# Two feed-forward layers behind agent attention, float32: the first block's second-layer products in full fp32, the block of 448 tokens second, and part of the late weights' decoding on GpSimd

## The chip, the cores and the metric

One NeuronCore of a Trainium2 chip runs the whole kernel. The metric is the device time of one execution in microseconds. Names: TensorE (PE in the profile; PEld is its weight load), VectorE (DVE), ScalarE (ACT), GpSimd (POOL), SyncE (SP, which issues all DMAs of this kernel).

## What is computed

12480 tokens of 128 channels, 49 agents, two feed-forward layers with 2048 hidden units. In short:

```python
agent_v = sm(agents, k) @ v                       # softmax over the 12480 keys
x = sm(q, agents) @ agent_v                       # softmax over the 49 agents
h = x @ w_in1;  g = where(h >= 1, h, where(h <= -1, 0, (h + 1)**2 / 4));  y = g @ w_out1
h = y @ w_in2;  g = s * relu(h)**2 + b;           out = g @ w_out2
```

Inputs and outputs are float32; the four weight matrices arrive as 64-bit floats, seen as pairs of 32-bit words.

## The kernel before

**Blocks and steps.** Tokens go through in 25 blocks whose widths stand in `widths`: 256, then 23 of 512, then 448. Tokens are the columns. A layer's block is worked in 8 steps (`JP`) of two chunks of 128 hidden units, so a step's tile is 128 x 2w. Layer-1 step n is block n // 8; layer 2 runs `D` = 11 steps behind layer 1.

**One step.** `H` makes the hidden values in PSUM. `relu`, `square` (ScalarE) and, in layer 1, `cap` (VectorE, L745) make g. Products run in fp32r, so g is split: `hi` rounds it to fp32r (`gh`, on ScalarE L754 or VectorE L756, chosen by `PAT1`, `PAT2`) and `lo` subtracts (`gl`, VectorE, L761). `O` sums three products per chunk, `wh*gh + wl*gh + wh*gl`, in one PSUM bank (`y` for layer 1, `o` for layer 2). A step for which `short` is true skips `hi` and `lo`, and `O` takes one product in full fp32 with the unsplit weights (`w32`) per chunk; before, these are the layer-1 steps below `FP` = 12. In the records a full fp32 product stands as two matmuls.

**First-layer scores.** The first layer's input weights and the attention's values are fused ahead (`weights`, `awh`, `awl`, L599 to L606), so that `H` of layer 1 takes the softmax over the agents directly. Blocks 0 and 1 (`t < QB`) take two products per chunk with `awh` and `awl`; later blocks take one (L707) and four small tiles side by side (L715), for which `px` is filled by DMA. From block 3 on, softmaxes are made for two blocks at a time: `pair_scores`, a transpose on VectorE (`pair_turn`, L266), the `pair_steps`, and at their end `spread`, which issues 32 DMAs on SyncE out of `turned` (L293). The next pair's transpose writes `turned` again and so waits for them.

**Weights.** `decode` turns eight pieces of 1024 columns (A: second output weights, B: first input, C: first output, D: second input) into float32 in six steps, numbered 0 to 5: `scale_down` (L364 or L368), `tail` (L373), `join` (L378), `sign` (L383), `high` (L389), `low` (L392). All eight are scaled on ScalarE (`MACT`); all `low` run on VectorE.

**Order.** Each engine takes its instructions in the order in which the program issues them. Up to the fused weights that order is written out in `SEQ`, from there to layer-1 step 13 in `RAMP` (tokens: `H0` is layer 1's H, `h0` layer 2's, `R S M O` relu, square, cap and output product of layer 1, `r s G l o` those of layer 2, `A0.5` step 5 of piece A0, `z` a step of an early block's softmax, `=F1`, `=G1` high and low part of a quarter of the fused weights, `x` a column sum of the second output weights). Behind that `steady` weaves the lists in `PAIR`, one for each engine, under the dependencies given to `add`. `LOADS` is the order of the loads; the loads of keys and values share seven buffers, those of weight pieces three.

Of the kernel before, what the change touches and what calls it, by code (L numbers as in the profile page):

```python
# [18 lines left out]
def kernel(  # L19
# [55 lines left out]
        "B0 k0 k1 k2 k3 k4 k5 k12 k6 k7 k8 k9 k10 k11 v0 q0 v1 v2 v3 C1 v4 C0 B1 v5 v6 v7 q1 v8 v11 v9 v10 D0 "  # L75
        "v12 A0 q2 A1 D1"
    )
    RAMP = (
# [5 lines left out]
    )  # L84
    MACT = "B0 C1 C0 B1 D0 A0 A1 D1".split()
    WORD = "B0 C1 C0 B1 D0 A0 A1 D1".split()
    NR, FP = 14, 12
# [14 lines left out]
    widths = [256] + [512] * 23 + [448]  # L102
# [44 lines left out]
    w32, turned = shared[:, :DFF], shared[:, 2 * TB:]  # L147
    ptok = [packed[:, i * TB:(i + 1) * TB].rearrange("p (c n) -> p c n", n=P) for i in range(NPT)]
# [119 lines left out]
    def pair_steps(v):  # L268
# [10 lines left out]
        def spread():  # L279
# [4 lines left out]
            for j, t in enumerate(x for x in pair_blocks(v) for _ in range(2)):  # L284
# [6 lines left out]
                for dst, main in ((pt_t[t], True), (px_t[t], False)):  # L291
                    for c in range(4):
                        nc.sync.dma_start(  # L293
                            out=dst.bitcast(F32)[c * RG:(c + 1) * RG, x0:x0 + n], in_=src[:, c if main else 4]
                        )
# [51 lines left out]
    def decode(dec, src, dst, dst_h, dst_l, name):  # L347
# [12 lines left out]
        def scale_down():  # L360
            if not t:
                begin()
            if name in MACT:
# [3 lines left out]
            else:  # L367
                nc.vector.tensor_scalar_mul(t["y"].bitcast(F32), t["hi"].bitcast(F32), 2.0 ** -112)  # L368
# [22 lines left out]
        def low():  # L391
            nc.vector.tensor_tensor(  # L392
# [46 lines left out]
    def agents_values(pro, dec, wi1):  # L439
        pieces.update({  # L440
            "A": (w_out2, None, flat(wo2h), flat(wo2l)), "B": (w_in1, wi1, None, None),
# [11 lines left out]
        avt = pro.tile([P, P], F32, name="avt")  # L453
# [266 lines left out]
    def short(layer, n):  # L720
        return layer == 1 and n < FP
# [5 lines left out]

    def gv(d, layer, n):
        return d[layer, n][:, :, :blocks[n // JP][1]]

    def relu(layer, n):
        gx[layer, n] = ring("gl", layer, n, F32, GR) if short(layer, n) else ring("x", layer, n, F32, XB)
# [40 lines left out]
    def last_step(first):  # L773

        n = NS - 1
        if first:
            gx[2, n] = ring("x", 2, n, F32, XB)
# [11 lines left out]
    def O(layer, n):  # L789
# [6 lines left out]
        if short(layer, n):  # L796
            x = gx.pop((layer, n))
            ops = [(w32.rearrange("p (k d) -> p k d", d=P), x)]
# [65 lines left out]
    def steady():  # L864
# [19 lines left out]
        for n0 in range(NR, NS + D + D2 + 2, 2):  # L884
            for e, tokens in (PAIR if n0 < NS else TAIL).items():
                for token in tokens:
# [20 lines left out]
                    elif c == "o" and 0 <= m - 2 < NS:  # L907
                        k = m - 2
                        add(("o", k), [("l", k), ("Z", k // JP - 1)], O, 2, k)
# [14 lines left out]
                    elif c == "r" and 0 <= m < NS - 1:  # L924
                        add(("r", m), [("h", m), ("l", m - XB)], relu, 2, m)
# [4 lines left out]
                    elif c in "GC" and 0 <= m - 1 < NS - 1 and (c == "G") == (GH(2, m - 1) == "1"):  # L930
# [66 lines left out]
```

## Time and profile before

| | |
|---|---|
| median of 3 runs | 1059.88 us (1059.49 to 1060.31) |
| the profiled execution | 1058.94 us, of it the span of its instructions 1057.2 us |
| PE busy | 1039.0 us (98%) |
| DVE busy | 965.9 us (91%) |
| ACT busy | 980.5 us (93%) |
| POOL busy | 0.9 us, 7 instructions |
| granted TensorE clock, mean | 0.996 |

The span runs from the first to the last instruction. Matmuls are pipelined: one shows a duration longer than the time to the next one's start, and an engine that is busy throughout may still lose time, so starts are compared. "Idle" in brackets is the engine's idle time ahead of an instruction and what ended it.

### The profile page before, as it was taken

What the parts mean: (1) busy time and instruction counts of PE and PEld (TensorE: products, weight loads), DVE (VectorE), ACT (ScalarE), POOL (GpSimd) and SP (SyncE); (2) the same over time, 40 slices, a digit from 0 to 9 for tenths busy, and PEclk for the clock granted to TensorE, in tenths of its full rate; (3) what the DMA queues carried; (4) which work ended last, traced back from release to release, by engine and by line L of the source; (5) the groups of instructions that cost most, each with busy time, mean ns of one, the idle gap of its engine ahead of it and who ended that gap; (6) DMA issues with size and microseconds to landing.
All of it is one profiled execution on the core that took longest, in us unless ns stands there. A gap on an engine that the chain in (4) does not pass through costs nothing.

```text
span 1057.2 us, 13302 instructions
## 1 busy us (share of the span) xinstructions
PE 1039.0 (98%) x4928; PEld 789.9 (75%) x4928; DVE 965.9 (91%) x1102; ACT 980.5 (93%) x1059; POOL 0.9 (0%) x7
## 2 busy tenths in 40 slices
PE   7899999999999999999999999999999999999998
PEld 3767667777777777777777777777777777777787
DVE  5698989999999999999999999999999999999876
ACT  3798989999999999999999999999999999999986
POOL 0000000000000000000000000000000000000000
PEclk9999999999999999999999999999999999999999
DMA  9940020110110110010010010020020010010000
GB/s 362 385 148 27 14 53 11 34 37 11 26 46 11 24 47 11 22 49 11 20 52 11 18 54 11 14 56 11 13 56 10 12 39 11 11 38 11 1 11 20
DMA packets 32114, 47.68 MB, mean 45 GB/s; under 512 B 7285, under 2 KB 23653, under 8 KB 31409
## 3 DMA queue, kind: packets, MB, share of 16 engines
q1 hardware_dynamic: 32049, 46.83, 14.0%
q8 instruction: 39, 0.64, 0.3%
q14 instruction: 26, 0.21, 0.1%
HBM read 27.58 MB, written 6.39 MB: 32 GB/s over the span
## 4 chain that ended last, share of the span: by engine, by line
PE 90%; DMA 3%; DVE 2%; ACT 2%; SPq 2%; issue 1%; DVEq 0%
PE y L805 26%; PE h L675 25%; PE o L805 24%; PE h L707 8%; PE h L715 4%; SPq L293 1%; DMA k<-in_kT 1%; DMA wu<-in_w_out 1%; PE qs L259 1%; DVE gl L761 1%; PE ks L510 1%; DMA px<-pt 1%; PE av L564 1%; DVE x L745 0%; ACT x L741 0%
## 5 line engine op out<-in xcount | busy, mean ns | idle before, releaser
L761 DVE TENSOR_TENSOR gl<-x,gh 128x1024 fp32r<-128x1024 f32 (+2 forms) x387 | 461.5, 1201 | 10.9 <-ACT gh L754 8.0
L741 ACT ACTIVATE x<-x 128x1024 f32<-128x1024 f32 (+2 forms) x387 | 405.6, 1048 | 11.5
L745 DVE SCALAR_TENSOR_TENSOR x<-h,x 128x1024 f32<-128x1024 f32 (+1 forms) x188 | 228.3, 1215 | 32.8 <-ACT x L741 32.5
L735 ACT ACTIVATE x<-h 128x1024 f32<-128x1024 f32 (+1 forms) x188 | 189.2, 1006 | 19.1 <-PE h L707 12.9
L737 ACT ACTIVATE x<-h 128x1024 f32<-128x1024 f32 (+2 forms) x199 | 197.0, 990 | 8.8 <-PE h L675 6.9
L756 DVE CAST gh<-x 128x1024 fp32r<-128x1024 f32 (+1 forms) x245 | 166.7, 681 | 15.5 <-ACT x L741 14.9
L675 PE MATMUL h<-yh,wi2h 128*128 128x512 f32 (+2 forms) x400 | 155.9, 390 | 1.7 <-ACT x L737 0.9
L805 PE MATMUL y<-gh,wo1h 128*128 128x512 f32 (+1 forms) x376 | 156.2, 415 | 0.0
L805 PE MATMUL o<-gh,wo2l 128*128 128x512 f32 (+2 forms) x400 | 155.5, 389 | 0.0
L675 PE MATMUL h<-yl,wi2h 128*128 128x512 f32 (+2 forms) x400 | 155.3, 388 | 0.0
L675 PE MATMUL h<-yh,wi2l 128*128 128x512 f32 (+2 forms) x400 | 155.3, 388 | 0.0
L805 PE MATMUL o<-gh,wo2h 128*128 128x512 f32 (+2 forms) x400 | 154.6, 387 | 0.0
L805 PE MATMUL o<-gl,wo2h 128*128 128x512 f32 (+2 forms) x400 | 154.0, 385 | 0.2 <-DVE gl L761 0.2
L754 ACT ACTIVATE gh<-x 128x1024 fp32r<-128x1024 f32 (+1 forms) x142 | 147.4, 1038 | 3.0
L805 PE MATMUL y<-gl,wo1h 128*128 128x512 f32 (+1 forms) x376 | 148.0, 394 | 0.5 <-DVE gl L761 0.5
L805 PE MATMUL y<-gh,wo1l 128*128 128x512 f32 (+1 forms) x376 | 147.8, 393 | 0.0
L707 PE MATMUL h<-pt,awm 128*128 128x512 f32 (+1 forms) x368 | 100.7, 395 | 0.3 <-ACT x L737 0.3
L805 PEld LDWEIGHTS y<-gh,wo1h 128*128 128x128 f32 x376 | 70.3, 187 | 33.1 <-issue 14.6
L675 PEld LDWEIGHTS h<-yh,wi2h 128*128 128x128 f32 x400 | 74.9, 187 | 20.2 <-ACT x L737 1.7
L805 PEld LDWEIGHTS o<-gh,wo2h 128*128 128x128 f32 x400 | 75.0, 188 | 17.3
L805 PEld LDWEIGHTS o<-gl,wo2h 128*128 128x128 f32 x400 | 75.2, 188 | 16.8 <-DVE gl L761 0.7
L675 PEld LDWEIGHTS h<-yh,wi2l 128*128 128x128 f32 x400 | 74.8, 187 | 17.2
(124 smaller groups left out, 852.2 us busy)
## 6 DMA issues: line engine op xcount, KB each, us to landing
k<-in_kT SPq DMA_DIRECT2D x12, 512.0 KB
v<-in_v_main SPq DMA_DIRECT2D x12, 512.0 KB, 11.5
out_T<-shared SPq DMA_DIRECT2D x23, 256.0 KB, 2.0
pt<-shared SPq DMA_DIRECT2D x172, 32.0 KB, 1.8
px<-shared SPq DMA_DIRECT2D x172, 32.0 KB, 1.8
qbuf<-in_qT SPq DMA_DIRECT2D x10, 512.0 KB, 3.5
wu<-in_w_in SPq DMA_DIRECT2D x4, 1024.0 KB, 11.2
wu<-in_w_out SPq DMA_DIRECT2D x4, 1024.0 KB
```

The lines of the kernel that those rows point to most:

```text
L259: nc.tensor.matmul(out=sc[j * RG:(j + 1) * RG, g], lhsT=a64[:, g * RG:(g + 1) * RG], rhs=qbuf[:, c0:c0 + QW].rearrange("p (b x) -> p b x", ...
L675: nc.tensor.matmul(out=h[:, i, :w], lhsT=a[:, sl], rhs=r, start=(m == 0), stop=(m == len(ops) - 1))
L707: nc.tensor.matmul(out=out[g], lhsT=awm[:, c * P:(c + 1) * P], rhs=pt_t[t][:, :w], start=not last, stop=last)
L715: nc.tensor.matmul(out=out[g], lhsT=awx[r, q], rhs=px_t[t][r, :w], start=not last, stop=last)
L735: nc.scalar.activation(out=x, in_=h, func=ACTF.Relu, scale=0.5, bias=0.5)
L737: nc.scalar.activation(out=x, in_=h, func=ACTF.Relu)
L741: nc.scalar.activation(out=x, in_=x, func=ACTF.Square)
L745: nc.vector.scalar_tensor_tensor(out=x, in0=h, scalar=1.0, in1=x, op0=ALU.max, op1=ALU.min)
L754: nc.scalar.activation(out=a, in_=x, func=ACTF.Copy)
L756: nc.vector.tensor_copy(out=a, in_=x)
L761: nc.vector.tensor_tensor(out=b, in0=x, in1=a.bitcast(F32), op=ALU.subtract)
L805: nc.tensor.matmul(out=o[:, :w], lhsT=l[:, c, :], rhs=r[:, i, :w], start=(c == 0 and m == 0), stop=(c == KF - 1 and m == len(ops) - 1),)
```

## The change

Five things:

- `short` is now also true for the layer-2 steps of block 0 (`FP2` = 8): no `hi` and `lo` there, and 16 products in full fp32 instead of 48 in fp32r. The second output weights are kept in float32 for it (`w32b`, into which A's `sign` writes). Behind these steps two of the three x buffers of layer 2 are the halves of `w32b`.
- The relu of layer 2 waits for an output product where its buffer was one of these (`before`), and `o` for `t` (the square) instead of `l`.
- `widths` starts 256, 448 and ends with 512.
- `SCALES` and `LOWS` give the engine of two decoding steps by piece, in the order of `PIECES`: A0, A1 and C1 are scaled on GpSimd, B0 on VectorE, the rest on ScalarE; A0, A1 and D0 have their low part subtracted on GpSimd, C0, C1 and D1 on VectorE.
- `SEQ`, `LOADS` and `RAMP` are written anew, with other places for most tokens; `avt` takes the memory of `swap`.

```diff
     LOADS = (
-        "B0 k0 k1 k2 k3 k4 k5 k12 k6 k7 k8 k9 k10 k11 v0 q0 v1 v2 v3 C1 v4 C0 B1 v5 v6 v7 q1 v8 v11 v9 v10 D0 "
-        "v12 A0 q2 A1 D1"
+        "k2 k0 B0 k1 k3 k4 k5 k12 k7 k6 k8 k9 k10 k11 v0 q0 v1 v2 v3 C1 C0 v4 B1 v5 v6 v7 q1 v8 v11 v9 v10 D0 "
+        "v12 A0 q2 D1 A1"
     )
     RAMP = (
-        "H0 =F2 =G1 =F3 z1.6 H1 =G2 =G3 K H2 R0 S0 z1.7 R1 S1 M0 H3 z1.8 R2 S2 O0 R3 A0.3 z1.9 M1 M2 H4 A0.4 S3 "
...
-        "M12 g12 R13 z2.9 S13 h0 X r0 s0 G0 M13 L12 h1 r1 g13 s1 O11 B h2 b p2 l0 r2 G1 o0 l1 P2"
+        "H0 =F3 =G1 z1.6 =F2 =G2 =G3 H1 K R0 S0 H2 M0 z1.7 H3 R1 S1 A0.3 R2 O0 M1 O1 R3 S3 S2 z1.8 z1.9 H4 A0.4 "
...
+        "z2.8 z2.9 R13 S13 g12 X h1 r1 r0 s1 L12 s0 M13 g13 O11 B p2 b h2 r2 o0 P2"
     )
-    MACT = "B0 C1 C0 B1 D0 A0 A1 D1".split()
+    SCALES, LOWS = "G G V S S G S S".split(), "G G V V V V G V".split()
+    PIECES = "A0 A1 B0 B1 C0 C1 D0 D1".split()
...
-    NR, FP = 14, 12
+    NR, FP, FP2 = 14, 12, 8
...
-    widths = [256] + [512] * 23 + [448]
+    widths = [256, 448] + [512] * 23
...
+    w32b = const.tile([P, DFF], F32, name="w32b")
...
-            if name in MACT:
+            on = SCALES[PIECES.index(name)]
+            if on == "S":
                 nc.scalar.activation(
                     out=t["y"].bitcast(F32), in_=t["hi"].bitcast(F32), func=ACTF.Copy, scale=2.0 ** -112
                 )
             else:
-                nc.vector.tensor_scalar_mul(t["y"].bitcast(F32), t["hi"].bitcast(F32), 2.0 ** -112)
+                by = nc.gpsimd if on == "G" else nc.vector
+                by.tensor_scalar_mul(t["y"].bitcast(F32), t["hi"].bitcast(F32), 2.0 ** -112)
...
-            nc.vector.tensor_tensor(
+            by = nc.gpsimd if LOWS[PIECES.index(name)] == "G" else nc.vector
+            by.tensor_tensor(
                 out=dst_l[:, sl], in0=t["f"], in1=dst_h[:, sl].bitcast(F32), op=ALU.subtract
             )
...
-            "A": (w_out2, None, flat(wo2h), flat(wo2l)), "B": (w_in1, wi1, None, None),
+            "A": (w_out2, w32b, flat(wo2h), flat(wo2l)), "B": (w_in1, wi1, None, None),
...
-        return layer == 1 and n < FP
+        return n < (FP if layer == 1 else FP2)
...
+    def x_ring(layer, n):
+        if layer == 1 or n % XB == XB - 1:
+            return ring("x", layer, n, F32, XB if layer == 1 else 1)
+        return w32b[:, n % XB * 2 * TB:(n % XB + 1) * 2 * TB].rearrange("p (b n) -> p b n", b=2)
...
-                        add(("o", k), [("l", k), ("Z", k // JP - 1)], O, 2, k)
+                        add(("o", k), [("t", k) if k < FP2 else ("l", k), ("Z", k // JP - 1)], O, 2, k)
...
-                        add(("r", m), [("h", m), ("l", m - XB)], relu, 2, m)
+                        before = [("o", m - GR) if m < FP2 else ("o", m - XB) if m < FP2 + XB else ("l", m - XB)]
+                        add(("r", m), [("h", m)] + before, relu, 2, m)
```

The new `SEQ` puts C1's scaling (`C1.0`, now GpSimd) right ahead of its join, `E12` ahead of `C1.5` and `t10`, and the second block's scores (`q1`) ahead of `a9`; its end is

```python
        "... q1 V12 a9 a10 V11 a11 a12 z1.0 z1.1 D0.1 n D0.0 T z1.2 H W0 z1.3 "
        "D0.2 z1.4 z1.5 W1 W2 F0 A0.0 D0.3 D0.4 A0.1 G0 W3 A0.2 F1"
```

## Rows read from the trace of the kernel before

**Rows 1.** Busy time by stretch of the span; columns by engine, then granted clock, DMA.

```profile
core 0: us, PE busy (x) PEld busy (x) DVE busy (x) ACT busy (x) POOL busy (x), PEclk, DMA share, GB/s
36.00:40.00 4.00, 3.45 (x44) 2.67 (x40) 4.00 (x7) 4.00 (x8) 0.00 (x0) 1.00 1.02 413
53.00:63.00 10.00, 7.44 (x30) 4.30 (x29) 9.97 (x18) 8.99 (x16) 0.00 (x0) 1.00 0.76 248
63.00:98.00 35.00, 34.98 (x179) 27.66 (x180) 32.14 (x45) 33.52 (x47) 0.00 (x0) 1.00 0.14 43
98.00:128.00 30.00, 28.30 (x158) 20.96 (x157) 29.24 (x40) 26.60 (x34) 0.00 (x0) 1.00 0.08 25
165.00:1020.00 855.00, 855.00 (x3909) 654.89 (x3908) 804.82 (x875) 823.90 (x844) 0.00 (x0) 1.00 0.09 25
```

**Rows 2.** Chain that ended last, in order of time: start us, us, what.

```profile
50.68 1.61 PE av L564 x20
53.57 2.00 PE aw L599 x4
83.53 1.72 PE y L805 x4
85.47 1.38 PE h L675 x12
93.79 6.68 DMA px<-pt
108.21 1.74 DVE gl L761 x2
140.89 1.88 DMA pt<-shared
167.22 1.40 PE h L675 x6
1042.37 1.24 PE o L805 x6
```

**Rows 3.** Timeline of PE: start us, us, instruction, idle before and what ended it.

```profile
58.70 0.39 PE L675 MATMUL h<-pt,awh 128*128 128x256 f32 x1 [0.95 <-DVE awl L606]
...
63.02 0.38 PE L675 MATMUL h<-pt,awh 128*128 128x256 f32 x1 [0.57 <-DVE gl L745]
...
99.70 0.50 PE L715 MATMUL h<-px,awx 19*128 19x512 f32 x3
100.51 0.50 PE L715 MATMUL h<-px,awx 19*128 19x512 f32 x1 [0.31 <-DMA px<-pt]
...
106.90 0.39 PE L675 MATMUL h<-yh,wi2h 128*128 128x256 f32 x1 [0.56 <-ACT x L737]
...
143.66 0.50 PE L675 MATMUL h<-yh,wi2h 128*128 128x512 f32 x1 [0.83 <-DVE shared L266]
...
145.99 0.50 PE L805 MATMUL y<-gl,wo1h 128*128 128x512 f32 x1 [0.20 <-DVE gl L761]
```

**Rows 4.** Waits (us in total, times, longest); SyncE's issues into pt, 90 to 146.

```profile
DVE shared L266 <- DMA pt<-shared: 3.9, 1, 3.9
...
L293 SPq DMA_DIRECT2D pt<-shared x16: 577/589/1370, 124.2 to 142.2; - x16
```

**Rows 5.** Groups by line and shape: count, busy us, mean ns, idle before.

```profile
L364 ACT ACTIVATE wt<-wu 128x1024 f32<-128x1024 f32 x8 | 9.3, 1157 | 1.2 <-DMA wu<-in_w_out 1.2
L761 DVE TENSOR_TENSOR gl<-x,gh 128x512 fp32r<-128x512 f32 x8 | 5.5, 683 | 1.1 <-ACT gh L754 1.1
L754 ACT ACTIVATE gh<-x 128x512 fp32r<-128x512 f32 x6 | 3.8, 628 | 0.1
L392 DVE TENSOR_TENSOR wi2l<-wt,wi2h 128x1024 fp32r<-128x1024 f32 x2 | 2.4, 1221 | 0.1
L756 DVE CAST gh<-x 128x512 fp32r<-128x512 f32 x2 | 0.8, 424 | 0.3 <-ACT x L741 0.3
L831 DVE TENSOR_SCALAR shared<-o,s_sb,bcol 128x448 f32<-128x448 f32 x1 | 0.7, 743 | 0.6 <-PE o L805 0.6
```

**Rows 6.** Groups of POOL, by line and shape.

```profile
masks.py:199 POOL TENSOR_SCALAR_AFFINE_SELECT ident<-ident 128x128 f32<-128x128 f32 x1 | 0.3, 292 | 0.1
```

More of the change, by code (lines that the diff above doesn't have):

```diff
@@ L290, in spread @@
                 src = turned[j * RG:(j + 1) * RG].rearrange("r (c x) -> r c x", x=QW)[:, :, QW - n:]
-                for dst, main in ((pt_t[t], True), (px_t[t], False)):
+                for dst, main in ((pt_t[t], True), (px_t[t], False)) if n else ():
                     for c in range(4):
@@ L452, in agents_values @@
         swap = pro.tile([P, P], F32, name="swap")
-        avt = pro.tile([P, P], F32, name="avt")
+        avt = swap
         sc, tp, tok, av, sw = {}, {}, {}, [], []
@@ L731, in relu @@
     def relu(layer, n):
-        gx[layer, n] = ring("gl", layer, n, F32, GR) if short(layer, n) else ring("x", layer, n, F32, XB)
+        gx[layer, n] = ring("gl", layer, n, F32, GR) if short(layer, n) else x_ring(layer, n)
         x, h = gv(gx, layer, n), gv(hp, layer, n)
@@ L776, in last_step @@
         if first:
-            gx[2, n] = ring("x", 2, n, F32, XB)
+            gx[2, n] = x_ring(2, n)
             gh[2, n] = ring("gh", 2, n, F32R, GR)
@@ L797, in O @@
             x = gx.pop((layer, n))
-            ops = [(w32.rearrange("p (k d) -> p k d", d=P), x)]
+            ops = [((w32 if layer == 1 else w32b).rearrange("p (k d) -> p k d", d=P), x)]
         else:
@@ L929, in steady @@
                         add(("t", m - 1), [("r", m - 1)], square, 2, m - 1)
-                    elif c in "GC" and 0 <= m - 1 < NS - 1 and (c == "G") == (GH(2, m - 1) == "1"):
+                    elif c in "GC" and FP2 <= m - 1 < NS - 1 and (c == "G") == (GH(2, m - 1) == "1"):
                         add(("g", m - 1), [("t", m - 1), ("o", m - 1 - GR)], hi, 2, m - 1, c == "G")
-                    elif c == "l" and 0 <= m - 1 < NS - 1:
+                    elif c == "l" and FP2 <= m - 1 < NS - 1:
                         add(("l", m - 1), [("g", m - 1), ("o", m - 1 - GR)], lo, 2, m - 1)
```

17 rows, old and new, of tables (RAMP, SEQ) are left out of this document.

## The prediction

> **What bounds the kernel now.** Start with the busy time by stretch [rows 1]. From 165 to 1020 us TensorE is busy for all of 855 us, VectorE for 804.8 and ScalarE for 823.9: there only TensorE's work counts. The stretch from 63 to 98 is the same (34.98 of 35.00). TensorE is short of full in two places: from 53 to 63 (7.44 of 10.00), and from 98 to 128 (28.30 of 30.00), where VectorE is at 29.24. Ahead of 53 the DMA engines are the limit, with ScalarE full beside them: from 36 to 40 their share is 1.02 and ScalarE has 4.00 of 4.00. Next read the chain that ended last, in order of time [rows 2]: a DMA into px from 93.8 to 100.5, then VectorE's subtractions (L761), then, with SyncE's 32 issues of the first pair's spread (L293) in between, the landing of a DMA of that spread at 142.8, and from there TensorE alone. So up to about 146 us other things than TensorE set the pace; behind that everything is a sum of its products. A microsecond saved ahead of 146 is saved at the end; one saved on VectorE or ScalarE later is worth nothing.
>
> The stops of TensorE [rows 3] say how much there is to win. Between 98 and 147 it stops seven times: once for px, three times for ScalarE's relu (L737), twice for VectorE's subtraction (L761), once for the pair's transpose (L266), which itself waits 3.9 us for the spread's DMAs [rows 4]; the first and the last of these and the pair's stand in the rows. The idle time shown is too small: a 512-column product shows 0.39 but the next one follows after 1.40/6 = 0.233 [rows 2], so each stop loses the idle time shown plus 0.16. At 143.66 that is 0.83 + 0.16, some 0.98. So the six stops other than px lose 0.73, 0.46, 0.39, 0.47, 0.98 and 0.37, together 3.4; the four ahead of 128 are 2.05 of it, the two behind are 1.35. The px stop is 100.51 - 99.70 = 0.8.
>
> **Second-layer products of block 0 in full fp32.** Removed: eight high parts (six on ScalarE at 0.63, two on VectorE at 0.42) and eight low parts on VectorE at 0.68 [rows 5]: ScalarE loses 3.8 us, VectorE 5.4 + 0.8 = 6.3, nearly all of it between 88 and 125, the stretch in which the chain runs through VectorE. Added: 16 products of full fp32 in place of 48. A step's two full products are four records, and at 512 columns these take 1.72 (the first layer's at 83.53 [rows 2]): 0.86 a product, so 0.43 at 256 columns. Three ordinary products of 256 columns take 3 x 1.38/12 = 0.345 [rows 2]. The difference is 0.085 x 16 = **+1.4** us of TensorE, with nothing to hide it.
>
> What the relief gives: the four stops ahead of 128 wait for VectorE or ScalarE, and both lose more work there (6.3 and 3.8) than the stops add up to (2.05). I take nine tenths, **-1.8**. The two stops behind 128 hang on the spread: SyncE needs 0.59 us for each of its 32 DMAs, the 16 for pt among them start from 124.2 to 142.2 [rows 4], and the next pair's transpose waits for the last that reads its place. With less on VectorE the spread comes earlier by up to 3 us while TensorE itself comes about 2 us earlier, so the gap of 1.35 mostly closes: **-1.1**, between 0 and -1.35. The px stop: the copy that feeds its DMAs stood on ScalarE behind two high parts of 0.63, which go; 1.26 earlier against a stop of 0.8, while TensorE also comes to that place a little sooner: **-0.5**, between 0 and -0.8. The new waits of relu for an output product instead of a low part (`("o", m - GR)`, `("o", m - XB)`) I cost at nothing: TensorE's list puts that product ahead of the H whose result the relu needs, so the second wait covers the first. Uncovered, one would cost a step's two products, 0.86.
>
> **Block of 448 second.** Between 512 and 448 columns an ordinary product differs by (1.40 - 1.24)/6 = 0.027 us [rows 2]. The second block has 32 products for its first-layer scores (later blocks 16, and 4 passes of four tiles at once). It saves 32 + 24 ordinary ones at 0.027 and eight full ones at 0.86 x 64/512 = 0.107: 2.37. The last block, now 512, gives back 16 + 4 + 48 at 0.027: 1.84. The second layer's cancels. Net **-0.5**. The drain behind the last product grows by the last evacuation, 0.74 for 448 columns [rows 5], so by 0.74/7: **+0.1**.
>
> **GpSimd's six instructions.** A0, A1 and C1 lose their scaling on ScalarE (1.16 each), B0's goes from ScalarE to VectorE, and A0, A1 and D0 lose their subtraction on VectorE (1.22 each) [rows 5]: 4.6 us off ScalarE, 3.7 off VectorE. Nothing in the trace shows GpSimd on 128x1024. The nearest rows are its own 128 columns in 0.29 us [rows 6], by which eight times as many take 2.3, and VectorE's 1.22 for the same shape [rows 5]. I take 2 us, nearer to its own row. It has free time throughout, so its own time costs nothing unless somebody waits. Who waits: VectorE's join of C1 (C1.2) behind C1.0, its join of A0 (A0.2) behind A0.0 with the low parts of the fused weights (awl, L606) queued behind that; the other results are needed ten or more microseconds later. The gain is at the start, where ScalarE is full (36 to 40) and its scalings stand between the exponentials: 1.16 us from C1. TensorE's last averages end at 52.3 and the fused weights start at 53.57 [rows 2], while the DMA engines are full; the bytes loaded ahead of the last values are the same. The averages themselves are 1.61 and what lies between them and the fused weights 1.3, so I let the start come at most 2.5 us sooner. I take **-1.0**, between +1 (C1.2 late on VectorE) and -2.5.
>
> From 53 to 63 TensorE stops for awl (58.70) and for VectorE's maximum (63.02), the first and the last of three [rows 3]; with some shorter ones beside them they lose 3.1. The new order puts all four low parts ahead of H1, which moves the same wait forward, and D0's subtraction leaves VectorE. Against that A0.2 waits for GpSimd. I take **0**, between -1.5 (half of the stops' 3.1) and +2.3 (one instruction of GpSimd). From 63 to 98 TensorE is full and stays so: 0.
>
> **The sum:** -1.0 (start) + 0 (53 to 63) - 0.5 (px) - 1.8 - 1.1 (stops) + 1.4 (full products) - 0.5 (widths) + 0.1 (drain) = -3.4. The profiled execution took 1058.94 (span 1057.2 and 1.74 around it), which gives 1055.5; the median of the runs is 0.94 above it, and carried over to that, 1059.88 - 3.4 = **1056.5**.
>
> **The rivals.**
> *The gain is given back.* TensorE reaches px and the pair's transpose sooner, but the DMAs don't land sooner: the px DMA takes 6.68 us of its own, the spread 20 us of SyncE. What is freed ahead of them is then waited for there. The chain speaks for it; against it, VectorE's work is in that same chain ahead of the spread. Left are -1.0 + 1.4 - 0.5 + 0.1 = 0: 1059.9.
>
> *GpSimd holds VectorE up (slower).* [...] Price: six instructions of 2.3 us, 13.8, against a relief of 6.3 + 3.7 = 10.0. VectorE comes to 98 us 3.8 us later than now instead of earlier, no stop goes, and the ones there grow: +1.4 - 0.5 + 0.1 + 3.8 = +4.8, or 1064.7. It decides from a hold of 10.0/6 = 1.7 us for each instruction. For it: VectorE is the fullest engine in both stretches. [...]
> [...]
>
> *More than forecast.* All stops from 98 go (-4.2), half of those from 53 to 63 (-1.5), and the start comes to the DMA's limit (-2.5), with +1.0 for the rest: -7.2, 1052.7.
>
> **How the numbers follow.** This kernel's runs can tell about 0.2%, 2.1 us, from no change: the bounds are 1057.8 and 1062.0. The forecast with its own spread (1055 to 1058.5) has 0.55, of which 0.50 lies below 1057.8. The given-back case has 0.25 (0.22 within, 0.03 above), the slower one 0.10 (0.08 above, 0.02 within), the larger gain 0.10. Faster 0.60, same 0.29, slower 0.11. The range takes in the given-back case and half of the larger one: 1053.4 to 1060.6.
>
> **What would show it.** Right: TensorE's stops for L737 and L761 between 98 and 128 are gone, the transpose (L266) of the second pair waits less than 3.9 us, 32 records of `o` with about 0.215 us from start to start stand in place of 48, and the steady stretch repeats as it is. GpSimd's rows say 1.2 to 2.3 us each, and VectorE's subtractions and joins beside them keep 1.22 us. Wrong: VectorE instructions of 2 us and more beside GpSimd's; a wait of A0.2 or C1.2 for GpSimd above 1 us with a stop of TensorE behind it; fused weights that start later than 53.6; a new stop at px or L266 as large as the ones that went.

## The result, and the profile of the kernel after

The kernel after takes **1065.12 us** (median; 1063.25 to 1065.63), the kernel before beside it 1059.43 (1059.15 to 1060.31): a ratio of 1.0051 with a 95% interval of 1.0041 to 1.0062, so slower by 5.7 us, where 3.4 faster was forecast. The profiled execution took 1064.90, with a span of 1063.1 against 1057.2 before. One execution of the last experiment below, at a mean granted clock of 0.654, took 1436 us and is left out of its numbers.

First the same stretches as in [rows 1] from 53 us on (columns as there):

```profile
core 0: us, PE busy (x) PEld busy (x) DVE busy (x) ACT busy (x) POOL busy (x), PEclk, DMA share, GB/s
53.00:63.00 10.00, 5.75 (x17) 2.97 (x16) 9.97 (x12) 4.90 (x10) 5.89 (x3) 0.92 0.70 233
63.00:98.00 35.00, 34.36 (x167) 28.41 (x168) 27.64 (x41) 30.45 (x45) 7.17 (x3) 0.92 0.15 45
98.00:128.00 30.00, 29.39 (x163) 23.62 (x162) 26.59 (x36) 25.25 (x32) 0.00 (x0) 1.00 0.08 25
165.00:1020.00 855.00, 855.00 (x3901) 653.51 (x3900) 805.47 (x875) 824.17 (x843) 0.00 (x0) 1.00 0.09 25
```

The stretch that was to be relieved was relieved: from 98 to 128 VectorE falls from 29.24 to 26.59, and TensorE rises from 28.30 to 29.39. But from 53 to 63 TensorE falls from 7.44 to 5.75 with VectorE as full as before, and VectorE now does 12 instructions there instead of 18. The granted clock is below 1 in the two stretches on either side of 63. TensorE's timeline (start us, us, instruction, idle before and what ended it; the lines of after for [rows 3]) shows the stops:

```profile
58.31 0.39 PE L680 MATMUL h<-pt,awl 128*128 128x256 f32 x1 [1.03 <-DVE awl L611]
61.72 0.58 PE L680 MATMUL h<-pt,awh 128*128 128x256 f32 x1 [2.79 <-DVE awl L611]
...
64.91 3.54 PE L815 MATMUL y<-gl,shared 128*128 128x256 f32 x8
...
103.79 0.50 PE L720 MATMUL h<-px,awx 19*128 19x512 f32 x1 [0.40 <-DMA px<-pt]
...
127.24 0.47 PE L815 MATMUL o<-gl,wo2h 128*128 128x448 f32 x1 [0.21 <-DVE gl L771]
128.97 0.73 PE L712 MATMUL h<-pt,awm 128*128 128x512 f32 x2 [0.18 <-ACT w32b L747]
...
145.29 0.47 PE L680 MATMUL h<-yh,wi2h 128*128 128x448 f32 x1 [2.09 <-DVE shared L268]
```

The wait for the low parts of the fused weights (awl) at 58.70 was 0.95 and is 2.79 now; the pair's transpose (L268, L266 before) stops TensorE for 2.09 instead of 0.83. Eight records of y at 256 columns take 3.54 at 64.91; before, four took 1.02 (at 61.42). What VectorE and GpSimd do meanwhile, from the timelines of the two engines in the kernel after:

```profile
54.33 2.13 DVE L387 SCALAR_TENSOR_TENSOR wt<-wu,wt 128x1024 uint32<-128x1024 uint32 x1
56.38 1.28 DVE L377 TENSOR_SCALAR wt<-wu 128x1024 uint32<-128x1024 uint32 x1
...
58.18 2.89 DVE L382 SCALAR_TENSOR_TENSOR wt<-wt 128x1024 uint32<-128x1024 uint32 x1
60.99 0.68 DVE L611 TENSOR_TENSOR awl<-aw,awh 128x512 fp32r<-128x512 f32 x1
...
63.72 1.21 DVE L387 SCALAR_TENSOR_TENSOR w32b<-wu,wt 128x1024 uint32<-128x1024 uint32 x1
...
54.28 2.83 POOL L372 TENSOR_SCALAR wt<-wu 128x1024 f32<-128x1024 f32 x1 [20.19 <-DVE qsm L199]
57.63 2.35 POOL L397 TENSOR_TENSOR wi2l<-wt,wi2h 128x1024 fp32r<-128x1024 f32 x1 [0.52 <-ACT wi2h L393]
62.30 2.85 POOL L372 TENSOR_SCALAR wt<-wu 128x1024 f32<-128x1024 f32 x1 [2.31 <-DMA wu<-in_w_out]
```

Three VectorE instructions run beside GpSimd's scaling of A0 and subtraction of D0, and each takes longer: D0's sign (L387) 2.13, a tail step (L377) 1.28 and A0's join (L382) 2.89. The same three on VectorE in the kernel before take 1.22, 0.69 and 1.22:

```profile
54.45 1.22 DVE L383 SCALAR_TENSOR_TENSOR wt<-wu,wt 128x1024 uint32<-128x1024 uint32 x1
55.58 0.69 DVE L373 TENSOR_SCALAR wt<-wu 128x1024 uint32<-128x1024 uint32 x1
...
56.83 1.22 DVE L378 SCALAR_TENSOR_TENSOR wt<-wt 128x1024 uint32<-128x1024 uint32 x1
```

That is 0.91 + 0.59 + 1.67 = 3.2 us, and the part of awl for which TensorE stops stands behind all three on VectorE.

A fourth such place comes later. Beside GpSimd's subtraction for A1 (78.76 to 81.17) VectorE's subtraction of a softmax's maximum (L194) takes 1.58 instead of 0.35. It is in the chain that ended last, and TensorE stops for 0.57 behind it, at 83.58. First the line of after, then that of before:

```profile
79.81 1.58 DVE L194 TENSOR_TENSOR qe<-qe,qm 128x196 f32<-128x196 f32 x1
```

```profile
76.48 0.35 DVE L192 TENSOR_TENSOR qe<-qe,qm 128x196 f32<-128x196 f32 x1
```

The lines for [rows 4] and [rows 6]: VectorE waits longer for the spread's DMAs than the 3.9 before, and GpSimd's groups (count, busy us, mean ns, idle before) have the six new instructions.

```profile
DVE shared L268 <- DMA pt<-shared: 4.6, 1, 4.6
```

```profile
L372 POOL TENSOR_SCALAR wt<-wu 128x1024 f32<-128x1024 f32 x3 | 8.5, 2845 | 52.2 <-DMA wu<-in_w_out 32.0 <-DVE qsm L199 20.2
L397 POOL TENSOR_TENSOR wo2l<-w32b,wo2h 128x1024 fp32r<-128x1024 f32 x2 | 5.0, 2512 | 11.0 <-ACT wo2h L393 11.0
L397 POOL TENSOR_TENSOR wi2l<-wt,wi2h 128x1024 fp32r<-128x1024 f32 x1 | 2.4, 2352 | 0.5 <-ACT wi2h L393 0.5
```

And the lines for [rows 2], of the chain that ended last (start us, us, what): VectorE's sign is in it now, the DMA into px starts 3.3 us later, and four records of the full second-layer products take 0.86.

```profile
54.42 2.04 DVE wt L387
...
97.07 6.68 DMA px<-pt
...
106.62 0.86 PE o L815 x4
```

The place of the loss is read from the start of the same product in both traces, going along the span. The table gives the kernel before and the difference to it, for after and for five of the experiments below ("products": full fp32 products alone, and so on). Between profiles the fused weights start up to a microsecond apart, so that row is to be taken off the ones under it.

| first product of | before, us | after | products | widths | GpSimd | products, spread | mended |
|---|---|---|---|---|---|---|---|
| the fused weights | 53.57 | -0.12 | +0.72 | +0.76 | +0.99 | +0.57 | +0.11 |
| the second hidden step (H1) | 58.70 | +3.02 | +0.73 | +0.76 | +3.73 | +0.58 | +0.85 |
| the last short output step of layer 1 (O11; the last of its four records) | 87.98 | +3.39 | +0.86 | -0.26 | +4.84 | +0.56 | +2.92 |
| px | 99.70 | +3.18 | +1.33 | -0.89 | +4.84 | +1.04 | +3.42 |
| the second pair's scores | 137.40 | +0.56 | -0.82 | -1.87 | +4.84 | -1.11 | +1.54 |
| layer 2 of the third block | 157.15 | +1.86 | -0.06 | -0.56 | +4.86 | -2.36 | +0.20 |
| the last pair's scores | 861.80 | +1.52 | -0.07 | -0.90 | +4.83 | -2.39 | +0.20 |
| (the end of the span) | 1057.15 | +5.97 | -0.06 | +3.54 | +4.89 | -2.33 | +0.26 |

For the kernel after: 3.1 lost from the fused weights to H1, 2.6 won back between px and the second pair's scores, 1.3 lost at the pair's transpose, 0.3 won back by 197 us, nothing from there to 862 us, and 4.45 lost behind it, in the last block.

### The profile page after: what moved, and what is told of

Its sections match the earlier page's. It is cut to its first block, busy times and chain, and to the rows that moved or that the text cites. A ratio compares the mean times of both kernels' runs of the same rounds, so it can differ in the third digit from the quotient of the medians.

```text
span 1063.1 us, 13259 instructions
## 1 busy us (share of the span) xinstructions
PE 1042.8 (98%) x4910; PEld 794.7 (75%) x4910; DVE 964.1 (91%) x1090; ACT 972.5 (91%) x1049; POOL 16.7 (2%) x13
## 4 chain that ended last, share of the span: by engine, by line
PE 91%; DMA 3%; DVE 3%; SPq 2%; issue 1%; ACT 0%; POOL 0%; DVEq 0%; POOLq 0%
PE y L815 27%; PE h L680 26%; PE o L815 25%; PE h L712 8%; PE h L720 4%; SPq L295 1%; DMA k<-in_kT 1%; DMA wu<-in_w_out 1%; PE qs L261 1%; DMA px<-pt 1%; DVE wt L382 1%; PE ks L515 0%; PE av L569 0%; DVE wt L387 0%; POOL wt L372 0%
## 5 line engine op out<-in xcount | busy, mean ns | idle before, releaser
L771 DVE TENSOR_TENSOR gl<-x,gh 128x1024 fp32r<-128x1024 f32 (+1 forms) x252 | 304.6, 1213 | 4.3 <-ACT gh L764 2.8
L751 ACT ACTIVATE x<-x 128x1024 f32<-128x1024 f32 (+1 forms) x252 | 266.7, 1058 | 7.8
L771 DVE TENSOR_TENSOR gl<-w32b,gh 128x1024 fp32r<-128x1024 f32 (+1 forms) x127 | 153.9, 1212 | 4.7 <-ACT gh L764 2.8
L815 PE MATMUL o<-gh,wo2l 128*128 128x512 f32 (+1 forms) x384 | 151.0, 393 | 0.0
L815 PE MATMUL o<-gh,wo2h 128*128 128x512 f32 (+1 forms) x384 | 150.1, 391 | 0.0
L815 PE MATMUL o<-gl,wo2h 128*128 128x512 f32 (+1 forms) x384 | 149.3, 389 | 0.2 <-DVE gl L771 0.2
L751 ACT ACTIVATE w32b<-w32b 128x1024 f32<-128x1024 f32 (+1 forms) x127 | 134.1, 1056 | 3.5
L747 ACT ACTIVATE w32b<-h 128x1024 f32<-128x1024 f32 (+1 forms) x127 | 127.8, 1006 | 6.9 <-PE h L680 5.6
L712 PE MATMUL h<-pt,awm 128*128 128x512 f32 x368 | 101.4, 397 | 0.2 <-ACT w32b L747 0.2
L764 ACT ACTIVATE gh<-w32b 128x1024 fp32r<-128x1024 f32 (+1 forms) x90 | 94.6, 1051 | 1.9
```

Source lines behind the costliest of these rows:

```text
L712: nc.tensor.matmul(out=out[g], lhsT=awm[:, c * P:(c + 1) * P], rhs=pt_t[t][:, :w], start=not last, stop=last)
L747: nc.scalar.activation(out=x, in_=h, func=ACTF.Relu)
L751: nc.scalar.activation(out=x, in_=x, func=ACTF.Square)
L764: nc.scalar.activation(out=a, in_=x, func=ACTF.Copy)
L771: nc.vector.tensor_tensor(out=b, in0=x, in1=a.bitcast(F32), op=ALU.subtract)
L815: nc.tensor.matmul(out=o[:, :w], lhsT=l[:, c, :], rhs=r[:, i, :w], start=(c == 0 and m == 0), stop=(c == KF - 1 and m == len(ops) - 1),)
```

## The experiments

### GpSimd alone, and its instructions one by one

The kernel before with only the engines of the decoding changed:

```diff
-    MACT = "B0 C1 C0 B1 D0 A0 A1 D1".split()
+    MACT = "C1 C0 B1 D0 A0 A1 D1".split()
+    SCG, LOG = "A0 A1 C1".split(), "A0 A1 D0".split()
...
+            if name in SCG:
+                nc.gpsimd.tensor_scalar_mul(t["y"].bitcast(F32), t["hi"].bitcast(F32), 2.0 ** -112)
...
+            (nc.gpsimd if name in LOG else nc.vector).tensor_tensor(
```

> The kernel before with the changed engines of the decoding alone: A0, A1 and C1 scaled and A0, A1 and D0 subtracted on GpSimd, B0 scaled on VectorE; order, widths and products as before. Theory (VectorE is held up beside GpSimd): VectorE's sign and join of late weights between 54 and 61 us take 2 to 3 us each instead of 1.22, the second product of the hidden layer (58.70 us before) comes 2.5 to 4 us later, and a part of that is lost again at px: 1061 to 1063. Rival (the loss is in the new order of the work, not in GpSimd): those VectorE rows stay at 1.22 and the time stays within 1 us of 1059.5. My forecast's term for this part was -1.0.

Measured: 1063.49 (1062.96 to 1064.05), ratio 1.0037 [1.0023, 1.0051], +4.0. Its timelines of VectorE, GpSimd and TensorE:

```profile
57.10 1.22 DVE L376 TENSOR_SCALAR wt<-wu 128x1024 uint32<-128x1024 uint32 x1
58.82 2.96 DVE L381 SCALAR_TENSOR_TENSOR wt<-wt 128x1024 uint32<-128x1024 uint32 x1
...
54.84 2.92 POOL L365 TENSOR_SCALAR wt<-wu 128x1024 f32<-128x1024 f32 x1 [20.96 <-DMA wu<-in_w_out]
58.34 2.35 POOL L395 TENSOR_TENSOR wi2l<-wt,wi2h 128x1024 fp32r<-128x1024 f32 x1 [0.59 <-ACT wi2h L392]
...
62.43 0.57 PE L678 MATMUL h<-pt,awh 128*128 128x256 f32 x1 [2.85 <-DVE awl L609]
```

The join is as slow beside D0's subtraction again (2.96), and H1 comes 3.73 - 0.99 = 2.7 us later. D0's sign keeps its length here (1.21, inside GpSimd's scaling of A0), and a small one of 128x4 takes 0.69 instead of 0.17: which instructions are held differs from run to run, but together it is 2.8 here and 3.2 in after. From H1 to O11 another 1.1 goes, 0.5 of it at a stop of TensorE behind the softmax subtraction (1.58 again, at 80.40) and 0.3 at one behind a tail step of 1.62. Nothing of the 3.8 comes back behind that. The rival, that the loss was the order's and not GpSimd's, falls for this part.

Next the kernel after with A0's scaling on ScalarE:

```diff
-    SCALES, LOWS = "G G V S S G S S".split(), "G G V V V V G V".split()
+    SCALES, LOWS = "S G V S S G S S".split(), "G G V V V V G V".split()
```

> The changed kernel with A0 alone scaled on ScalarE again; the other five stay on GpSimd. If the scaling of A0 is what makes VectorE late (D0's sign and A0's tail held, and the join pushed into GpSimd's subtraction for D0): sign 1.22, tail 0.69, the join starts ahead of the subtraction and takes 1.22, H1 at 59.5, no clock drop, 1060.5. If the subtraction for D0 holds the join whatever comes ahead: the join still takes over 2.5, H1 at 60.5 to 61, 1063. Order theory: no change, 1065.

Measured: 1061.82 (1060.49 to 1064.39), ratio 1.0022 [1.0013, 1.0032]: 3.3 us back. VectorE's sign, tail and join are at their old length, and H1 waits less:

```profile
54.33 1.22 DVE L387 SCALAR_TENSOR_TENSOR wt<-wu,wt 128x1024 uint32<-128x1024 uint32 x1
57.13 1.23 DVE L382 SCALAR_TENSOR_TENSOR wt<-wt 128x1024 uint32<-128x1024 uint32 x1 [0.34 <-ACT wt L367]
...
59.31 0.39 PE L680 MATMUL h<-pt,awh 128*128 128x256 f32 x1 [1.69 <-DVE awl L611]
```

And with D0's subtraction back on VectorE (`LOWS` with V for G at D0), A0's scaling staying on GpSimd:

> The changed kernel with D0's low part alone subtracted on VectorE again. Hold theory: the join takes 1.22 instead of 2.89, H1 at 60.0 instead of 61.7, 1062 to 1063 if the clock still falls for the shorter gap, 1061 if it doesn't; the sign and the tail stay at 2.1 and 1.3. If the scaling of A0 alone is to blame, the join is as late as now and H1 stays at 61.5. Order theory: no change, 1065.

Measured: 1063.11 (1062.46 to 1063.62), ratio 1.0034 [1.0022, 1.0046]: 2.0 back. Here the join takes 1.23 but has waited 0.61 for GpSimd's scaling, and the tail step beside that takes 1.70. Without A0's scaling there all of the 3.2 us of VectorE are back, without D0's subtraction about half (H1 comes 1.7 sooner than in after).

With nothing at all on GpSimd (`SCALES` "S S V S S S S S", `LOWS` all V) and everything else as after:

> The changed kernel with nothing on GpSimd: A0, A1 and C1 are scaled on ScalarE, all low parts are subtracted on VectorE; order, widths and full products stay. Hold theory (GpSimd holds VectorE's instructions with two SBUF operands just ahead of awl: D0's sign 2.13 instead of 1.22, A0's tail 1.28 instead of 0.69, A0's join 2.89 instead of 1.22, so awl 3 us late, TensorE idle, its clock at half from 61.4 to 68.2): these come back to 1.22 and 0.69, H1 starts at 59 to 59.5 instead of 61.72, no clock drop at 61, and the time falls by about 5, to 1060. Order theory (the new order puts H1 behind three of the low parts of the fused weights, and that alone makes TensorE idle): H1 stays later than 61, the clock falls, the time stays above 1063.

Measured: 1065.28 (1062.81 to 1066.69), ratio 1.0050 [1.0033, 1.0068], no better than after. VectorE's lengths are the old ones and H1 waits 1.70, but in the profiled execution the fused weights start at 56.99, 3.5 us later than in after. Of these, 2.0 are there already at C1's tail step (34.19 against 32.22), and at the first product of the queries' scores (26.32 against 24.35), which comes ahead of the first instruction that this edit moves: this execution started late. The other 1.6 come from the join of C1, which waits 2.79 for ScalarE's scaling where it waited 1.22 for GpSimd's: the new order puts that scaling right ahead of the join. The runs spread over 3.9 us. So this run does not tell what GpSimd costs; the two above and the one of GpSimd alone do.

### TensorE's clock behind the stop

Behind the stop of 2.79 the eight y records take twice as long. The windows of the kernel after give the granted clock (the number after the engines) as 0.55 and 0.59 from 61 to 69:

```profile
61.00:65.00 4.00, 3.15 (x13) 2.89 (x14) 4.00 (x9) 1.84 (x4) 2.70 (x1) 0.55 0.56 178
65.00:69.00 4.00, 4.00 (x16) 3.31 (x16) 2.95 (x6) 2.73 (x5) 1.18 (x2) 0.59 0.39 119
```

The trace has it at half (0.50) from 61.4 to 68.3 and again from 146.8 to 150.2, each time behind one of the two long stops. The test puts twelve products that nobody reads into the first gap:

```diff
-        "H0 =F3 =G1 z1.6 =F2 =G2 =G3 H1 K R0 S0 H2 M0 z1.7 H3 R1 S1 A0.3 R2 O0 M1 O1 R3 S3 S2 z1.8 z1.9 H4 A0.4 "
+        "H0 d d d d d d d d d d d d =F3 =G1 z1.6 =F2 =G2 =G3 H1 K R0 S0 H2 M0 z1.7 H3 R1 S1 A0.3 R2 O0 M1 O1 ..."
```

> The changed kernel with twelve additional 128x512 products on TensorE, into a bank that nobody reads, between H0 and H1, about 2.8 us of work that the gap hides. VectorE is as late as before, H1 starts at 61.7 to 62. If half the clock behind the gap costs time of its own, the granted clock stays at full there, the eight records of O0 and O1 follow at 0.215 instead of 0.427 us, H4 comes 3 us behind the kernel before instead of 5, and the time falls by about 2, to 1063. If TensorE's speed behind the gap doesn't matter (VectorE and ScalarE being as late anyway), the time stays at 1065.

Measured: 1064.26 (1063.72 to 1065.18), ratio 1.0045 [1.0027, 1.0063]. The clock stays at 1.00 from 57 to 73:

```profile
58.13 2.93 PE L634 MATMUL warm<-packed 128*128 128x512 f32 x12
62.30 0.38 PE L680 MATMUL h<-pt,awh 128*128 128x256 f32 x1 [1.25 <-DVE awl L611]
```

H4 then comes 1.0 us sooner than in after, but O11 at +3.36 against +3.39: what sets O11 is not the clock. In both profiles VectorE's long L194 at 79.8 stands in between, with a stop of TensorE at 83.6. The 0.9 us by which this kernel is ahead at the end appear at the pair's transpose, where the clock stays full in this profile; that is also within the spread of the runs. So in this pair of profiles the half clock costs 0 at the first stop and at most about 0.9 at the second. But in the runs of after the time goes with the mean granted clock: it took 1063.25 in the one run at 0.993 and 1064.90 to 1065.63 in the five at 0.990 to 0.991. Where the clock fell in the runs without a profile is not on record, so a cost of one or two microseconds stays possible.

### The widths

The kernel before with `widths = [256, 448] + [512] * 23`, and the kernel after with the old `[256] + [512] * 23 + [448]`:

> The kernel before with the block of 448 second instead of last, and nothing else. Theory (the two ends do not cancel): the last block is all TensorE, so 512 columns instead of 448 there cost the 4.45 us that every kernel so far with the new widths lost behind 863 us; the second block saves about as much work, 5 us, but half of it is lost again in the waits for the px DMA and for the first pair's spread, so about 1062 (+1.5 to +4). Rival (my forecast): the second layer's share cancels and -0.5 is left, about 1059.

> The kernel after with the block of 448 last, as before, and nothing else undone. Theory (the two ends do not cancel): 4.45 us come back behind 863 us and 1 to 3 us are lost ahead of 165, so 1061 to 1063. Rival (they cancel): the kernel after's 1065.1 plus 0.5, 1065.5.

Measured: the widths alone 1061.23 (1060.31 to 1062.61), ratio 1.0018 [1.0008, 1.0027], +1.7; after with the old widths 1062.14 (1061.53 to 1062.63), 1.0025 [1.0015, 1.0034], 3.0 less than after. My forecast was -0.4 with the drain. The last pair's scores and the span, first in after and then in after with the old widths (x16 are the 16 products, then first and last start):

```profile
core 0 of [0], span 1063.1 us
L261 PE MATMUL qs<-qbuf,a x16: 379/379/403, 863.3 to 864.0; 128*32 128x256 f32 x16
```

```profile
core 0 of [0], span 1060.4 us
L261 PE MATMUL qs<-qbuf,a x16: 379/379/403, 865.0 to 865.7; 128*32 128x256 f32 x16
```

From there to the end it is 199.8 with a last block of 512 and 195.4 with 448: 4.4 us, the same in every kernel with either width. What the second block saves is in the table: the widths alone take 0.76 + 0.90 = 1.7 off, from the fused weights to the last pair's scores (all of it by 237 us). The rest went into waits. TensorE's two longest waits from 98 to 165 in the widths alone (us in total, times, longest):

```profile
PE h L675 <- DVE shared L266: 2.3, 1, 2.3
PE h L715 <- DMA px<-pt: 0.9, 1, 0.9
```

Before, the same view says 0.8 for the pair's transpose and 0.3 for px: both grew, by 2.1 together, because TensorE came there 0.89 and 1.87 us sooner (the table's rows for px and for the second pair's scores), while the DMA into px landed only 0.31 sooner (100.16 against 100.47) and the last of the spread that the transpose needs only 0.57 (142.20 against 142.77).

### The full products, and the spread that takes their gain

The kernel before with the full fp32 products of block 0 alone (the parts of the change with `FP2`, `w32b`, `x_ring` and `before`):

> The kernel before with the full fp32 second-layer products of the first block alone: the order of the work, the widths and the engines of the decoding stay as before. My forecast's terms for this part: stops -1.8 and -1.1, px -0.5, products +1.4, together -2.0: about 1057.5. Rival (the gain is given back at the px DMA and the spread): +1.4 - 0.5 and nothing else, about 1060.4, with the stop ahead of the second pair's transpose grown by 1 us or more.

Measured: 1058.25 (1057.70 to 1058.90), ratio 0.9987 [0.9978, 0.9996]: 1.3 us faster. From 98 to 165 TensorE waits:

```profile
PE h L680 <- DVE shared L268: 1.6, 1, 1.6
PE y L815 <- DVE gl L771: 0.2, 1, 0.2
```

The stops for px, for relu and for the low parts ahead of 128 are gone, as forecast; that for the pair's transpose is 1.6 instead of 0.8. VectorE itself stands 4.47 us ahead of that transpose, for a DMA that reads `shared`. SyncE starts its 32 issues at 123.61 here and at 124.21 before [rows 4], mostly at 0.63 from one to the next, so the last that the transpose needs lands as late as ever (at 142.71 against 142.77).

If that is the cause, issuing first the eight DMAs that read the place which the next transpose overwrites (parts 0 and 1 of `turned`) must free it. In the kernel after:

```diff
+            sends = []
...
-                        nc.sync.dma_start(
-                            out=dst.bitcast(F32)[c * RG:(c + 1) * RG, x0:x0 + n], in_=src[:, c if main else 4]
-                        )
+                        k = c if main else 4
+                        sends.append((k > 1, j, dst, c, x0, n, src, k))
+            for _, _, dst, c, x0, n, src, k in sorted(sends, key=lambda x: x[0]):
+                nc.sync.dma_start(out=dst.bitcast(F32)[c * RG:(c + 1) * RG, x0:x0 + n], in_=src[:, k])
```

> The kernel after, but the first pair's spread issues the eight DMAs that read what the next pair's transpose overwrites first, ahead of the other 24. Theory: the second pair's transpose, which lost 2.25 us of TensorE at 143 to 145 and was followed by 3.4 us at half the granted clock, then waits for nothing, so 2.5 to 4 us come back: about 1062. Rival: the stop only moves to the next reader of the spread or to the second-layer products, and the time stays within 0.5 us of 1065.1.

Measured: 1063.18 (1060.78 to 1065.89), ratio 1.0035 [1.0023, 1.0046], 1.9 less than after; the stop at the transpose is gone and so is the half clock behind it. It is less than the 2.5 to 4 expected, and the runs spread over 5 us, along with their mean granted clock: 1060.78 to 1061.73 at 0.994 to 0.995 (the profiled one among them), 1063.14 to 1065.89 at 0.990 to 0.992. A cleaner measure is the same edit on the products alone:

> The kernel before with the full fp32 second-layer products of the first block (as in the run of these products alone, 1058.25) and with the first pair's spread reordered, so that the eight DMAs that read what the next pair's transpose overwrites go first. Theory (the products' gain is given back at the spread): the stop ahead of the second pair's transpose, 1.74 us at 141.6 us in that run, is gone, and the time is 1.3 to 2 us shorter, 1056.2 to 1057.0. Rival (a later reader of the same DMAs takes the wait over): within 0.5 us of 1058.25.

Measured: **1056.71** (1056.08 to 1057.97), ratio 0.9975 [0.9965, 0.9985]: 1.5 less than the products alone, and faster than both kernels. SyncE's timeline (x10: ten issues for pt in a row, where four for pt and four for px took turns) shows the new order; from 98 to 165 the view of waits has no line for TensorE any more:

```profile
123.31 6.29 SPq L299 DMA_DIRECT2D pt<-shared  x10
```

On top of it the new widths, to see whether the second block's saving comes through once VectorE and the spread leave room:

> The same as the run with the products and the reordered spread, but with the block of 448 second instead of last. Theory (what the second block saves is only won where TensorE sets the pace): with VectorE relieved and the spread no longer waited for, the second block saves 4 to 5 us ahead of 165 and the last block gives 4.45 back, so within 1 us of the run with the old widths. Rival (the second block's saving is lost whatever stands around it, as in the run of the widths alone, +1.7): 1.5 to 3 us slower than with the old widths.

Measured: 1058.47 (1057.07 to 1059.87), ratio 0.9990 [0.9981, 0.9998], 1.8 slower than with the old widths. My theory expected a tie; the rival came true. At the last pair's scores it stands 4.88 us ahead of the kernel before, where the one with the old widths stands 2.39 ahead, and it started 0.4 later than that one: the second block saves 2.9 us here, more than the 1.7 of the widths alone, but not the 4.4 that the last block costs. TensorE's longest wait from 98 to 165 is again for the spread, whose px parts the reordering left at the end of the queue:

```profile
PE h L722 <- DMA px<-shared: 0.6, 1, 0.6
```

### What the new order costs

The kernel after with the three causes taken out: `SCALES` "S G V S S G S S" and `LOWS` "G G V V V V V V", the old widths, the reordered spread.

> The kernel after, with the three causes found so far taken out at once: A0 scaled on ScalarE and D0 subtracted on VectorE (so that nothing of GpSimd runs from 54 to 61 us), the block of 448 last again, and the first pair's spread reordered; the new order, the full products and GpSimd's other four instructions stay. Theory (these causes are the loss): 1065.1 - 3.3 (A0, D0) - 3.0 (widths) - 1.3 to 2 (spread) = 1056.8 to 1057.5. Rival (the new order of the work costs by itself): 1059 or more.

Measured: 1059.04 (1058.67 to 1059.60), ratio 0.9996 [0.9988, 1.0005]: 6.1 back, but 2.3 more than the same products and spread in the old order. The rival was right: something is left. Two candidates, GpSimd's other instructions and the order; the next takes all of GpSimd away but for C1's scaling (`SCALES` "S S V S S G S S", `LOWS` all V):

> The mended kernel after (1059.04), with three more instructions taken off GpSimd: A1's scaling goes to ScalarE, A0's and A1's subtractions to VectorE; only C1's scaling is left on GpSimd. Theory (GpSimd holds VectorE up wherever TensorE waits for VectorE; here VectorE's tail step, 2.25 us instead of 0.69 at 67 us, and the stop of 0.99 us behind it): the stops from 63 to 84 us go, 1057 to 1058. Rival (the new order of the work costs by itself): within 0.5 us of 1059.0.

Measured: 1059.27 (1058.48 to 1060.45), ratio 0.9995 [0.9986, 1.0004], no difference: the rest is the **order's**. (B0's scaling on VectorE, the other thing that is new in both, lies ahead of the fused weights, and these start no later, at 53.68 and 54.36 against 54.15 in the old order.) TensorE's longest stops in this kernel, from its timeline:

```profile
60.22 0.38 PE L682 MATMUL h<-pt,awh 128*128 128x256 f32 x1 [1.70 <-DVE awl L613]
61.88 0.36 PE L682 MATMUL h<-pt,awh 128*128 128x256 f32 x1 [0.92 <-DVE awl L613]
```

In the old order with the same products and spread these are 0.96 and 0.62. The new order sets F0 ahead of A0's scaling; with that scaling on ScalarE the join comes later (in the first mended kernel it waits 0.35 us for ScalarE, from 57.0 to 57.37), and with the scaling on GpSimd it is held up instead. This is 1.0 of the 2.3 to 2.6 us. The rest goes by O11, and the two profiles lose it differently: the first mended kernel has a stop of 0.99 at 67.20, behind a tail step of 2.25 beside GpSimd, and this one, without that, has 3.4 us at half the granted clock from 62.55. That part was not taken apart.

Last, the first term of my sum by itself: the old order, products and reordered spread, with C1's scaling alone on GpSimd.

> The kernel with the full products and the reordered spread in the order of before (1056.71), with C1's scaling on GpSimd and nothing else there: the first term of my sum (the start) alone. Forecast: the fused weights' products start 1.0 us sooner and the time is 1.0 us shorter, 1055.7. Rival (the start hangs on the DMA engines, not on ScalarE's scaling): within 0.4 us of 1056.7, and slower by up to 1 us if VectorE's join of C1 waits for GpSimd.

Measured: 1056.61 (1056.40 to 1057.92), ratio 0.9976 [0.9967, 0.9985]: 0.1 from the kernel without it. VectorE's join of C1 waits 2.16 us for GpSimd, and the fused weights start at 54.52 against 54.15: nothing clear is won or lost by it.

## Why the prediction was wrong, point by point

The sum was -3.4; the result was +5.7. The steps in their order:

- **The start, -1.0: wrong, about 0.** C1's scaling alone gives -0.1. ScalarE was full from 36 to 40, but relieving it moved nothing; the DMA engines are full beside it (1.02 [rows 1]), and I had named that limit and still took a gain. That they are the reason is likely but not shown: no run relieved them.
- **53 to 63, 0 within -1.5 to +2.3: this step failed most.** It cost 3.1 at H1. The upper bound was one instruction of GpSimd; but two stand there back to back, and three instructions of VectorE, each longer by 0.6 to 1.7 in the kernel after, lie in front of the same awl. The list of who waits had named the right place, "A0.2 behind A0.0 with awl queued behind", and then priced only the wait for the result, not VectorE's own slowing. The new order was also written for A0's scaling on GpSimd: with this back on ScalarE it still loses 2.3 to 2.6.
- **63 to 98, 0: a little off, the same way.** From H1 to O11 0.4 more goes in after and 1.1 with GpSimd alone, where the softmax subtraction of 1.58 stands in the chain.
- **The rival "GpSimd holds VectorE up" was right in kind, at the wrong place and price.** I priced six instructions of 2.3 us each, felt at 98, and a hold of 1.7 as the point from which it decides. Measured in after are lengthenings of 0.6 to 1.7 at 54 to 61, where VectorE is full and TensorE waits for it; there a few of them are enough, while C1's scaling at 31 costs nothing. That the rival's 1064.7 lies so near to 1065.12 is luck: its sum has the widths at -0.4 where they cost 1.7, leaves out the order, and gets its 3.8 for GpSimd from six instructions held for 2.3 each less 10.0 of relief, which no run shows. I had overlooked the sign, tail and join that stand between the awl parts; a chance of 0.10 was too low. Of my signs of being wrong two came: VectorE instructions above 2 us beside GpSimd's, and a larger stop at the transpose.
  The overlaps in after are not alike. The join ends 1.09 us after D0's subtraction (61.07 against 59.98), about its own length of 1.22; but the sign of 2.13 ends at 56.46, ahead of GpSimd's 57.11, and that at 63.72 takes 1.21 inside GpSimd's 62.30 to 65.15. So here the measurement shows a hold in some overlaps and none in others; what decides between them was not shown.
- **Stops ahead of 128, -1.8: right.** In the products alone none of the four is left; in after there is one short one, 0.21 of idle time, and another of 0.18 just behind 128.
- **The px stop, -0.5: too much.** In the products alone the stop of 0.8 is gone, but TensorE also comes to px 1.33 - 0.72 = 0.6 later there, counted from the fused weights, so the product behind the stop starts only 0.2 sooner. In after the stop is 0.9 (103.79 against 102.88). There the DMA into px starts at 97.07 instead of 93.79 [rows 2], as late as everything else.
- **Stops behind 128, -1.1: wrong, the other way.** The pair's transpose costs 2.25 instead of 0.98. I let the spread come 3 us earlier with a relieved VectorE; it came 0.6 earlier in the products alone and, with the late start of the steps ahead, at 125.79 in after. This is the rival "the gain is given back", and it is right for this term: the reordered spread returns 1.5 us.
- **Full products, +1.4, and with the stops -2.0 in all: right in sign.** The records are the 0.215 us apart that were forecast (0.86 for four); the part is worth -1.3 alone, and -2.8 with the spread reordered.
- **Widths, -0.5 and drain +0.1: wrong, +1.7.** "The second layer's cancels" was the step. It cancels in work: 96 products at 0.027 are 2.6 at either end, which makes 1.84 + 2.6 = 4.4 for the last block, as measured, and 2.37 + 2.6 = 5.0 for the second. But the last block's 4.4 us are all on the path, and the second block's saving lies ahead of px and the spread, where DMAs end the waits: 1.7 of it comes through alone, 2.9 at best.
- **The steady stretch: right.** 855.00 of 855.00, and the differences between the kernels stand still from 237 to 862 us.

The parts alone are -1.3 (products), +1.7 (widths), +4.0 (GpSimd) and, from the mended kernels, +2.3 to +2.6 (order), together 6.7 to 7.0 against 5.7; GpSimd and the order share the wait for awl, so they don't add up in full.

## What to carry to other kernels

A width that was moved here between a stretch where everything waits for TensorE and one where TensorE waits for DMAs counted in full at the first and only in part at the other: 64 columns of work left the second block, which saved 1.7 to 2.9 us of 5.0, and came to the last one, which cost 4.4. So price both ends of such a move by which wait ends last there, not by work. An engine with free time was not free to use: beside GpSimd's work three instructions of VectorE took 3.2 us longer in after. So ask which instructions of its neighbour stand beside it, and whether someone waits for those. And a hand-written order belongs to the engines that it was written for; try parts of a change alone, as here one of four was worth keeping, and it wanted one more edit, the order of 32 DMA issues.

## What the runs showed of the hardware

- GpSimd takes 2.8 to 2.9 us in after to scale 128x1024 and 2.4 to 2.6 to subtract two of them, where ScalarE and VectorE take 1.16 and 1.22 [rows 5]. I had taken 2. It can be the one that is held: the scaling of A0 took 3.88 with D0's subtraction on VectorE and with the gap filled, and there the sign, issued 0.1 us ahead of it, kept its 1.22.
- Beside GpSimd, VectorE's two-input join takes up to 3.42 us instead of 1.22, and its one-input tail step up to 2.87 instead of 0.69 (both with the gap filled); in the mended kernel (timelines of the three engines below) the tail takes 2.25, with a stop of TensorE behind it. The softmax subtraction takes 1.58 instead of 0.35. Most others in such overlaps keep their length: in after the tail step at 32.22 takes 0.69 inside GpSimd's 31.23 to 34.09, and the sign at 63.72 takes 1.21.

```profile
67.06 2.25 DVE L379 TENSOR_SCALAR wt<-wu 128x1024 uint32<-128x1024 uint32 x1
...
65.97 2.79 POOL L399 TENSOR_TENSOR wo2l<-w32b,wo2h 128x1024 fp32r<-128x1024 f32 x1
...
67.20 0.39 PE L682 MATMUL h<-pt,awh 128*128 128x256 f32 x1 [0.99 <-DVE gl L757]
```

- In after, stops of 2.79 and 2.09 us went with 6.8 and 3.4 us at half the granted clock; with the first gap filled by products there was none, at either place. A stop alone does not tell: in the filled-gap profile the transpose's stop of 2.17 at 145.36 is followed by the full clock, and behind the same stop of 0.96 ahead of H1 the products alone have 3.4 us at half the clock (from 60.92) and the products with the reordered spread have none.
